# Turning the second norm's rows with VectorE squares and transfers in a transformer block on one NeuronCore

## The chip, the cores and the metric

The kernel runs on one core of a Trainium2 chip. The metric is the device time of one execution in microseconds. Three runs of the kernel before took 1683.07, 1687.08 and 1701.88 us; their median is 1687.08 us.

## What is computed

The reference is one transformer block with adaptive layer norm: attention with 32 query heads of 16 columns that share one head of keys and values, and a dense layer with relu. There are 2048 rows of 512 float32 columns and 1792 hidden columns.

```python
mod = (_silu(c) @ w_mod).reshape(c.shape[0], 6, 1, -1)
sa, ca, ga, sb, cb, gb = (mod[:, 0], mod[:, 1], mod[:, 2], mod[:, 3], mod[:, 4], mod[:, 5])
h = _layernorm(x, axis=-1) * (1 + ca) + sa
x = x + ga * _A_ref(h, A_wq, A_wk, A_wv, A_wo)     # softmax(q k^T / 4) v, then wo
h = _layernorm(x, axis=-1) * (1 + cb) + sb         # the second norm
x = x + gb * _B_ref(h, B_w1, B_w2)                 # relu(h w1) w2
```

## The kernel before

**Attention.** The main loop (`for c in range(NU * KT // 2)`, near the end of `build`) runs 256 cycles. A unit `u` is a block of 256 query rows with a group of 8 heads; there are 32 units of 16 key tiles, and a cycle takes two key tiles of one unit, so that 8 cycles are a unit and 32 cycles a block of 256 rows. In a cycle TensorE computes eight tiles of scores (`scores`, into one of three `ps_exp` banks), which ScalarE exponentiates into `pe`; eight tiles of scores of a later unit (`max_of`, into one of three `ps_max` banks), whose row maxima VectorE takes; and, at the end of each of the two parts of the cycle, the products with the values (`values`, into `ps_pv`). Once a unit, VectorE forms `negm` and its transpose `sq`, ScalarE and Pool split it (`ms`), and SP sends it through DRAM into the rows of `qp` that the next unit's scores read (`mdr<-ms`, `qp<-mdr`).

**Order.** The schedule is manual: each engine runs its instructions in the order in which the program issues them, and the strings `PARTS` give that order within the two parts of a cycle: `c` and `d` are scores, `a` and `b` maxima, `u` and `l` the work behind attention, `t` the turns. After the fourth letter of the first part the list `put_off` is run: splits on ScalarE and Pool that were put off from the cycle before.

**Work behind attention.** From the second block of cycles on, the generator `behind(b)` supplies in portions, one a cycle, what follows attention for the block before: the output projection, the second norm, the dense layer. Seven blocks are done this way; the last one comes after the loop in `behind_last`, with code of its own. Most of a portion's matmuls are issued in halves of 64 rows (`on_half`) beside the score matmuls, which use the other half of the array.

**The second norm.** For a block, `x1` holds two tiles of 128 rows. The sums of tile 0 (`ln_sums`) come during the projection. `second_norm` is stepped once a cycle, at the cycle's end, during the portions of `fill` (the second half of the dense layer of the block before; in the first block a projection of queries and four empty portions). Its first step takes the sums of tile 1 (`bn_stats`, `bn_aggr`) and starts the reciprocal square root, three operations on VectorE and 13 small ones on Pool; the second step normalises both tiles on Pool into `xn` (six operations of 128x512). Portions 4 and 5 each bring a turn: `turned_too` lets TensorE transpose four squares of 128x128 by the identity into a `ps_exp` bank, the upper halves of the rows in the first part of the cycle and the lower halves in the second (`in_two`). ScalarE copies the bank to a stage tile, and in the next cycle `split` makes its two parts `hh` (ScalarE) and `hl` (Pool), which the dense layer reads from portion 7 on.

Of the kernel before, what the change touches and what calls it, by code (L numbers as in the profile page):

```python
# [9 lines left out]
F32 = mybir.dt.float32  # L10
# [8 lines left out]
S, D, H, DH, DFF = 2048, 512, 32, 16, 1792  # L19
P = 128  # L20
LB = 512
NL = S // LB
TB = 256
NB = S // TB
TT = TB // P
DC = D // P
# [10 lines left out]

PARTS = "cbcuaucuautcuau", "tbldldladbllbld"  # L40
SYNC = mybir.DependencyInfo(mybir.DependencyClass.Sync, mybir.DependencyReason.DATA)
MANUAL = {ET.PE, ET.Activation, ET.DVE, ET.Pool, ET.SP}

# [13 lines left out]
def build(tc, nc, cst, sb, ps, dr, x, wq, wk, wv, wo, w1, w2, c, w_mod, out):  # L57
# [8 lines left out]
    def ps_fill():  # L66
        return ps.tile([P, 512], F32, name="ps_fill", tag="fill", bufs=1)
# [46 lines left out]
    cols = cst.tile([P, 2, DC], F32, name="cols")  # L114
# [91 lines left out]
    def ln_sums(mv, t, src):  # L206
        st = sb.tile([P, 6], F32, name="st", tag="st", bufs=2)
        nc.vector.bn_stats(st, src)  # L208
        nc.vector.bn_aggr(mv[:, t], st)
# [29 lines left out]
    def split(hi, lo, src, eng=None):  # L239
        nc.scalar.activation(hi, src, AF.Copy)  # L240
        (eng or nc.gpsimd).tensor_tensor(lo, src, hi.bitcast(F32), op=OP.subtract)  # L241

    def stage():
        return sb.tile([P, 512], F32, name="stg", tag="stg", bufs=3)

    def split_psum(hi, lo, pt, func=AF.Copy, stg=None, **kw):
        stg = stage() if stg is None else stg
        nc.scalar.activation(stg, pt, func, **kw)  # L248

        def parts():  # L250
            split(hi, lo, stg)

        return parts


    put_off = []
# [122 lines left out]
            qps[u].append(t.rearrange("p a n -> p (a n)"))  # L379


    later, turns = [], []

    negms = [cst.tile([P, 32], F32, name=f"negm{n}") for n in range(2)]
    for negm in negms:
# [69 lines left out]
    def turned(src, k2, pt):  # L455

        return [("turn", pt[:, (k * TT + t) * P:(k * TT + t + 1) * P],
                 src[:, t, (k2 * 2 + k) * P:(k2 * 2 + k + 1) * P])
                for k in range(2) for t in range(TT)]

    def flat(t, k2):
        return t[:, k2 * 2:k2 * 2 + 2].rearrange("p a n -> p (a n)")
# [17 lines left out]
    def normed(x1, xn, ts, nm, y, eng):  # L480
        for n, t in enumerate(ts):
            eng.tensor_scalar(xn[:, t], x1[:, t], nm[:, n:n + 1], y[:, n:n + 1],
                              op0=OP.add, op1=OP.mult)
            eng.tensor_tensor(xn[:, t], xn[:, t], cbr, op=OP.mult)
            eng.tensor_tensor(xn[:, t], xn[:, t], sbr, op=OP.add)
# [25 lines left out]
    def behind(b):  # L511
        def in_parts(todo, n):
            for i in range(0, len(todo), n):
                yield todo[i:i + n]

        def turned_too(src, parts, k2, bank):

            def turn():
                pt = bank()

                def end():
                    put_off.append(split_psum(flat(parts[0], k2), flat(parts[1], k2), pt))

                return turned(src, k2, pt), end

            turns.append(turn)

        def second(b, t):
            pt = ps_fill()
            yield from in_parts(dense2(b, t, pt), 6)  # L530
            ot = sb.tile([P, D], F32, name="ot", tag="tmp", bufs=2)
            add_psum(ot, pt, x1s[b][:, t])
            nc.sync.dma_start(out[b * TB + t * P:b * TB + (t + 1) * P], ot)

        x1, oo = open_block(b)
        if b == 0:
            qqs = [sb.tile([P, 2, LB], F32R, name="qq", tag="w1s", bufs=3) for _ in range(2)]
            rest, fill = [others_of(14 + n, qqs[n]) for n in range(2)]
            fill = itertools.chain(fill, [[]] * 4)
        else:  # L540
            rest, fill = carried.pop(), second(b - 1, 1)
        yield next(rest)
        yield next(rest)
        for k2 in range(DC // 2):
            put_off.append(partial(split, flat(oo[0], k2), flat(oo[1], k2), flat(on[b], k2)))
        yield from rest
        xn = sb.tile([P, TT, D], F32, name="xn", tag="xn", bufs=1)
        mv = ln_mv(TT)
        for t in range(TT):
            pt = ps_fill()  # L550
            for n, part in enumerate(in_parts(out_proj(pt, oo, t), 6)):
                yield part
                if t and n == 0:
                    ln_sums(mv, 0, x1[:, 0])
            add_psum(x1[:, t], pt, x1[:, t])
        ahead = [load_w1(f) for f in range(2)]

        def second_norm():
            ln_sums(mv, 1, x1[:, 1])
            stats = ln_stats(mv, TT, False)  # L560
            yield
            normed(x1, xn, range(TT), *stats, nc.gpsimd)
            yield

        norm2 = second_norm()
        hp = [sb.tile([P, DC, TB], F32R, name=n, tag="t4", bufs=2) for n in ("hh", "hl")]
        for n, part in enumerate(fill):
            if n in (4, 5):
                turned_too(xn, hp, n - 4, ps_exp)
            yield part  # L570
            next(norm2, None)
        r4 = r4s[b] = [sb.tile([P, 8, TB], F32R, name="r4", tag="big", bufs=4) for _ in range(4)]
        for f2 in range(FC // 2):
            pt = ps_fill()
            for f in range(f2 * 2, f2 * 2 + 2):
                if f + 2 < FC:
                    ahead.append(load_w1(f + 2))
                yield dense1(pt[:, (f % 2) * TB:(f % 2 + 1) * TB], ahead.pop(0), hp)
            i, f = divmod(f2 * 2, 8)
            put_off.append(split_psum(  # L580
                r4[i * 2][:, f:f + 2].rearrange("p a n -> p (a n)"),
                r4[i * 2 + 1][:, f:f + 2].rearrange("p a n -> p (a n)"), pt, AF.Relu))
        first_half = second(b, 0)
        yield from itertools.islice(first_half, 4)
        carried.append(first_half)
# [206 lines left out]

        return [back, partial(nc.gpsimd.tensor_tensor, on[b][:, g], num, den, op=OP.mult)]

    def in_two(turn):

        begun = []

        def first_part():
            begun.extend(turn())  # L800
            for d in begun[0]:
                on_half(d, 1)

        def second_part():
            for d in begun[0]:
                on_half(d, 0)
            begun[1]()

        return first_part, second_part

    def run(g):
        for _ in g:
            pass
# [71 lines left out]
    for c in range(NU * KT // 2):  # L885
        s = c * 2
        todo_of = dict(
            c=[partial(scores, *n) for n in ((s, 0), (s, 2), (s + 1, 0), (s + 1, 2))],
            d=[partial(scores, *n) for n in ((s + 2, 1), (s + 2, 3), (s + 3, 1), (s + 3, 3))
               if n[0] < NU * KT])  # L890
        if places:
            u, i, j = places.pop(0)
            todo_of.update(a=[partial(max_of, u, 0, i, j, kb) for kb in range(KB)],
                           b=[partial(max_of, u, 1, i, j, kb) for kb in range(KB)])
        for parts, load in later:
            put_off.append(parts)
            ends.append((c, load))
        later.clear()
        if not portion:

            pt = ps_fill()
            portion = [("f32r", pt, kp[:, 0:P], kp[:, 0:512], n == 0, n == 5) for n in range(6)]
        halves = [in_two(turn) for turn in turns]
        turns.clear()
        own = []
        for h in range(2):
            each = [partial(on_half, d, h) for d in portion]
            cuts = [len(each) * k // 6 for k in range(7)]
            own.append([partial(in_turn, each[x:y]) for x, y in zip(cuts, cuts[1:])])
        own[0].append(advance)  # L910
        todo_of.update(l=[partial(in_turn, own[0][k:k + 1 + k // 5]) for k in range(6)], u=own[1])
        for part in range(2):
            todo_of["t"] = [partial(in_turn, [half[part] for half in halves])]
            for n, what in enumerate(PARTS[part]):
                if todo_of.get(what):
                    todo_of[what].pop(0)()
                if part == 0 and n == 3:
                    in_turn(put_off)
                    put_off.clear()
            values(s + part)  # L920
        for due in [end for end in ends if end[0] <= c]:
            ends.remove(due)
            due[1]()  # L923
        next(todo, None)
        if c == NU * KT // 2 - 2:
            opened = open_last(NB - 1)
        if c and c % 32 == 0:
            assert next(others, None) is None
            others = behind(c // 32 - 1)
            portion = next(others)  # L930
# [31 lines left out]
```

## Time and profile before

| | before |
|---|---|
| median of three runs | 1687.08 us |
| lowest and highest run | 1683.07, 1701.88 us |
| profiled execution, its span | 1690.2 us |
| granted TensorE clock, mean | 0.994 |
| DMA, mean over the span | 77 GB/s |
| DMA packets | 88080 |

The time of the profiled execution beside its span is not given; the span is 3.1 us above the median of the runs and lies among them. In a row of the profile, `L879 PE MATMUL ps_pv<-pe,vt` is line 879 of the kernel, a matmul on TensorE that reads the tiles `pe` and `vt` and writes `ps_pv`. In the timeline a row begins with its start and its length in microseconds, `x4` says that four alike were merged, and the brackets give the idle time of the engine before the row and what ended it. PE is TensorE, DVE VectorE, ACT ScalarE, POOL GpSimd, SPq the queue from which SyncE issues transfers.

### The profile page before, as it was taken

The numbers are of one execution on the slowest core, as the hardware profiler recorded it, in microseconds if no ns is written. First come the engines' busy times: TensorE is split into PE (matmuls) and PEld (weight loads), VectorE is DVE, ScalarE is ACT, GpSimd is POOL, SyncE is SP. The second block draws the span as 40 slices with busy tenths as digits, with TensorE's granted clock in tenths as the row PEclk, the third lists the DMA queues.
The fourth block names the chain that finished last, engine by engine and source line by source line (L and its number), as shares of the span: only waits on it lengthen the run. The fifth ranks groups of instructions, "written<-read, shape, count | busy, mean of one in ns | idle before, by whom it ended". The sixth has DMA issues, their size and how long they took to land.

```text
span 1690.2 us, 34028 instructions
## 1 busy us (share of the span) xinstructions
PE 1666.9 (99%) x13130; PEld 922.0 (55%) x13130; DVE 1373.7 (81%) x2336; ACT 1228.0 (73%) x2399; POOL 345.2 (20%) x433
## 2 busy tenths in 40 slices
PE   7999999999999999999999999999999999999999
PEld 5444444445654565546654565546654565546668
DVE  7788888888888888888889888888889888888031
ACT  4238888777877778778877787778877777778830
POOL 3103355331102311121102211131103111131110
PEclk9899999999999999999999999999999999999999
DMA  8024643312301131113301131103311131103331
GB/s 288 30 62 138 199 127 102 92 60 79 101 19 48 45 104 54 36 41 96 92 25 39 47 107 49 59 17 97 91 29 35 47 115 40 61 16 100 108 121 57
DMA packets 88080, 129.86 MB, mean 77 GB/s; under 512 B 25140, under 2 KB 52724, under 8 KB 87920
## 3 DMA queue, kind: packets, MB, share of 16 engines
q1 hardware_dynamic: 86208, 127.55, 24.6%
q8 instruction: 105, 1.72, 0.4%
q14 instruction: 55, 0.45, 0.1%
q10 hardware_dynamic: 1712, 0.13, 0.1%
HBM read 100.33 MB, written 25.15 MB: 74 GB/s over the span
## 4 chain that ended last, share of the span: by engine, by line
PE 93%; DVE 3%; issue 1%; ACT 1%; DMA 1%; POOL 0%; POOLq 0%; DVEq 0%; ACTq 0%
PE ps_pv L879 30%; PE ps_exp L753 21%; PE ps_fill L163 18%; PE ps_max L426 18%; PE ps_exp L146 2%; PE ps_max L146 1%; DVE pm L428 1%; PE ps_exp L307 1%; PE ps_fill L146 1%; DVE st L208 1%; PE ps_exp L293 1%; DMA wmod<-in_w_mod_dram 1%; PE ps_exp L190 0%; PE ps_exp L159 0%; PE ps_fill L190 0%
## 5 line engine op out<-in xcount | busy, mean ns | idle before, releaser
L428 DVE TENSOR_REDUCE pm<-ps_max 128x1 f32<-128x512 f32 x2048 | 1292.5, 684 | 191.8 <-PE ps_max L426 145.6
L755 ACT ACTIVATE pe<-ps_exp 128x512 f32<-128x512 f32 x2048 | 1081.1, 605 | 301.6 <-PE ps_fill L163 137.2
L426 PE MATMUL ps_max<-kp,qp 48*128 48x512 f32 x2048 | 805.0, 439 | 7.6 <-DVE pm L428 7.5
L753 PE MATMUL ps_exp<-qp,kp 50*128 50x512 f32 x2048 | 723.7, 412 | 3.5 <-ACT pe L755 3.4
L879 PE MATMUL ps_pv<-pe,vt 128*32 128x512 f32 x4096 | 545.5, 605 | 0.0
L426 PEld LDWEIGHTS ps_max<-kp,qp 48*128 48x128 f32 x2048 | 364.0, 185 | 264.5 <-DVE pm L428 237.4
L753 PEld LDWEIGHTS ps_exp<-qp,kp 50*128 50x128 f32 x2048 | 358.7, 185 | 271.5 <-ACT pe L755 179.9
L163 PE MATMUL ps_fill<-w2r,r 64*128 64x512 f32 x1044 | 302.9, 405 | 0.0
L163 PE MATMUL ps_fill<-hh,w1s 64*128 64x256 f32 x1568 | 242.9, 285 | 0.0
L163 PEld LDWEIGHTS ps_fill<-hh,w1s 64*128 64x128 f32 x1568 | 216.9, 186 | 13.9 <-PEq L156 6.7
L163 PEld LDWEIGHTS ps_fill<-w2r,r 64*128 64x128 f32 x1044 | 180.7, 185 | 11.8 <-PEq L156 2.5
L879 PEld LDWEIGHTS ps_pv<-pe,vt 128*32 128x32 f32 x4096 | 80.6, 108 | 142.6 <-issue 122.3
L241 POOL TENSOR_TENSOR r<-stg,r 128x512 fp32r<-128x512 f32 x49 | 62.9, 1283 | 321.9 <-ACT r L240 321.9
L163 PE MATMUL ps_fill<-hT,wq 64*128 64x256 f32 x416 | 128.3, 405 | 0.0
L163 PE MATMUL ps_fill<-hl,w1s 64*128 64x256 f32 x784 | 126.4, 280 | 0.0
L163 PEld LDWEIGHTS ps_fill<-hl,w1s 64*128 64x128 f32 x784 | 105.2, 185 | 0.0
L923 POOL TENSOR_TENSOR on<-num,den 128x256 f32<-128x256 f32 x31 | 22.8, 734 | 232.5 <-DMA den<-recs 160.1
L163 PEld LDWEIGHTS ps_fill<-hT,wq 64*128 64x128 f32 x416 | 68.3, 185 | 2.8
L769 POOL COPY num<-pvs 128x256 f32<-128x256 f32 x32 | 12.7, 398 | 179.3 <-ACT pvs L765 179.3
L241 POOL TENSOR_TENSOR hl<-stg,hh 128x512 fp32r<-128x512 f32 x14 | 18.0, 1284 | 133.1 <-ACT hh L240 133.1
L261 POOL TENSOR_TENSOR x<-stg,x 128x512 f32<-128x512 f32 x14 | 18.1, 1291 | 99.2 <-ACT stg L260 99.2
L248 ACT ACTIVATE stg<-ps_fill 128x512 f32<-128x512 f32 x62 | 38.2, 616 | 0.0
(147 smaller groups left out, 927.6 us busy)
## 6 DMA issues: line engine op xcount, KB each, us to landing
w1s<-w1dr SPq DMA_DIRECT2D x104, 512.0 KB
qdr<-qq SPq DMA_DIRECT2D x48, 256.0 KB
qp<-qdr SPq DMA_DIRECT2D x128, 96.0 KB
raw<-in_B_w_dram SPq DMA_DIRECT2D x28, 256.0 KB
w1dr<-w1s SPq DMA_DIRECT2D x14, 512.0 KB
wmod<-in_w_mod_dram SPq DMA_DIRECT2D x6, 1024.0 KB
x<-in_A_x_dram SPq DMA_DIRECT2D x8, 512.0 KB
out_dram<-ot SPq DMA_DIRECT2D x16, 256.0 KB
```

The lines of the kernel that those rows point to most:

```text
L146: nc.tensor.matmul(pt, w, a, start=start, stop=stop)
L163: ins = nc.tensor.matmul(pt, w[r], a[r], start=start and h == 1, stop=stop and h == 0)
L208: nc.vector.bn_stats(st, src)
L241: (eng or nc.gpsimd).tensor_tensor(lo, src, hi.bitcast(F32), op=OP.subtract)
L248: nc.scalar.activation(stg, pt, func, **kw)
L261: nc.gpsimd.tensor_tensor(dst, stg, other, op=OP.add)
L426: nc.tensor.matmul(pt, qps[u][i][r, j * P:(j + 1) * P], kp[r, kb * 512:(kb + 1) * 512], start=True, stop=True)
L428: nc.vector.tensor_reduce(pms[u][:, (i * 2 + hf) * 4 + j, kb:kb + 1], pt, axis=AX.X, op=OP.max)
L753: nc.tensor.matmul(pt, kp[r, kt * P:(kt + 1) * P], qps[u][ct // 2][r], start=True, stop=True)
L755: nc.scalar.activation(pe, pt, AF.Exp)
L879: nc.tensor.matmul(pvt[i * 32:(i + 1) * 32], vt[:, kt], pes.pop((s, i)), start=(kt == 0), stop=(kt == KT - 1))
L923: due[1]()
```

## The change

The turns on TensorE go: `turned_too`, `in_two` and the letter `t` are taken out, and so is the copy through the stage tile. `second_norm` gets more steps, one at the end of each cycle of `fill`: `bn_stats` of tile 1; `bn_aggr` and the start of the reciprocal square root; the normalising on Pool; VectorE's transpose of tile 0; its transpose of tile 1 and the 32 transfers; the two splits, put off to the next cycle. VectorE's `transpose` turns each square of 32x32 in place, so that `xt` holds the right squares at the wrong partitions. For each tile, 16 transfers on SP's queue bring row `i` and column `j` of the squares to where they belong in `xh`: each moves 32 partitions of four pieces of 32 float32. `xh` takes the tag `xn`, which has one buffer, and `xt` the tag `tmp`, which has two.

```diff
-PARTS = "cbcuaucuautcuau", "tbldldladbllbld"
+PARTS = "cbcuaucuaucuau", "bldldladbllbld"
...
         def second_norm():
-            ln_sums(mv, 1, x1[:, 1])
+            st = sb.tile([P, 6], F32, name="st", tag="st", bufs=2)
+            nc.vector.bn_stats(st, x1[:, 1])
+            yield
+            nc.vector.bn_aggr(mv[:, 1], st)
             stats = ln_stats(mv, TT, False)
             yield
             normed(x1, xn, range(TT), *stats, nc.gpsimd)
+            yield
+            xts = [sb.tile([P, D], F32, name="xt", tag="tmp", bufs=2) for t in range(TT)]
+            for t in range(TT):
+                nc.vector.transpose(xts[t], xn[:, t])
+                if t == 0:
+                    yield
+            xh = sb.tile([P, DC, TB], F32, name="xh", tag="xn", bufs=1)
+            for t in range(TT):
+                rows = xts[t].rearrange("p (k j n) -> p j k n", k=DC, j=4)
+                cols = xh[:, :, t * P:(t + 1) * P].rearrange("p k (i n) -> p i k n", i=4)
+                for i, j in itertools.product(range(4), range(4)):
+                    nc.sync.dma_start(cols[j * 32:(j + 1) * 32, i], rows[i * 32:(i + 1) * 32, j])
+            yield
+            for k2 in range(DC // 2):
+                put_off.append(partial(split, flat(hp[0], k2), flat(hp[1], k2), flat(xh, k2)))
             yield
...
         for n, part in enumerate(fill):
-            if n in (4, 5):
-                turned_too(xn, hp, n - 4, ps_exp)
             yield part
             next(norm2, None)
...
-        halves = [in_two(turn) for turn in turns]
-        turns.clear()
...
-            todo_of["t"] = [partial(in_turn, [half[part] for half in halves])]
```

More of the change, by code (lines that the diff above doesn't have):

```diff
@@ L379, in load_q @@
             qps[u].append(t.rearrange("p a n -> p (a n)"))
-    later, turns = [], []
+    later = []
     negms = [cst.tile([P, 32], F32, name=f"negm{n}") for n in range(2)]
@@ L514, in in_parts @@
                 yield todo[i:i + n]
[L516 to L526, printed above, removed]
         def second(b, t):
@@ L793, in normalise @@
         return [back, partial(nc.gpsimd.tensor_tensor, on[b][:, g], num, den, op=OP.mult)]
[L795 to L809, printed above, removed]
     def run(g):
```

## The prediction

> **What bounds the kernel now.** First the page's busy shares and its chain of waits, columns as printed.
>
> ```profile
> span 1690.2 us, 34028 instructions
> PE 1666.9 (99%) x13130; PEld 922.0 (55%) x13130; DVE 1373.7 (81%) x2336; ACT 1228.0 (73%) x2399; POOL 345.2 (20%) x433
> PE 93%; DVE 3%; issue 1%; ACT 1%; DMA 1%; POOL 0%; POOLq 0%; DVEq 0%; ACTq 0%
> ```
>
> TensorE carries the chain. In the attention loop it, VectorE's row maxima and ScalarE's exponentials go in lockstep, so what counts is how long one cycle of the loop gets. A cycle is two parts, and each part ends with eight `ps_pv` matmuls. Next, then, the timeline of TensorE for the fourth block that runs behind attention: the `ps_pv` groups that close a cycle (start us, us, ...), and between them the turns that the change removes.
>
> ```profile
> 910.49 1.06 PE L879 MATMUL ps_pv<-pe,vt 128*32 128x512 f32 x8
> ...
> 916.49 1.06 PE L879 MATMUL ps_pv<-pe,vt 128*32 128x512 f32 x8
> ...
> 922.49 1.07 PE L879 MATMUL ps_pv<-pe,vt 128*32 128x512 f32 x8
> ...
> 929.12 1.06 PE L879 MATMUL ps_pv<-pe,vt 128*32 128x512 f32 x8
> ...
> 934.90 1.06 PE L879 MATMUL ps_pv<-pe,vt 128*32 128x512 f32 x8
> ...
> 940.68 1.06 PE L879 MATMUL ps_pv<-pe,vt 128*32 128x512 f32 x8
> ...
> 942.96 0.43 PE L159 MATMUL ps_exp<-idn,xn 64*128 64x64 f32 x4
> ...
> 947.36 1.06 PE L879 MATMUL ps_pv<-pe,vt 128*32 128x512 f32 x8
> ...
> 954.03 1.06 PE L879 MATMUL ps_pv<-pe,vt 128*32 128x512 f32 x8
> ...
> 959.82 1.06 PE L879 MATMUL ps_pv<-pe,vt 128*32 128x512 f32 x8
> ```
>
> An undisturbed cycle takes 5.78 us (934.90 to 940.68). Those that end at 947.36 and 954.03 hold the turns and take 6.68 and 6.67. The one that ends at 929.12 takes 6.63. VectorE's timeline says why:
>
> ```profile
> 911.59 0.68 DVE L208 BATCH_NORM_STATS2 st<-x 128x6 f32<-128x512 f32 x1
> 912.30 0.18 DVE L209 BATCH_NORM_AGGREGATE mv<-st 128x2 f32<-128x6 f32 x1
> ...
> 923.60 0.68 DVE L208 BATCH_NORM_STATS2 st<-x 128x6 f32<-128x512 f32 x1
> ...
> 924.94 0.17 DVE L222 TENSOR_SCALAR y<-y 128x2 int32<-128x2 int32 x1
> ...
> 948.42 0.22 DVE L432 TENSOR_REDUCE negm<-pm 128x16 f32<-128x64 f32 x1
> 948.75 0.21 DVE L392 STREAM_TRANSPOSE sq<-negm 128x32 f32<-128x32 f32 x1
> ```
>
> Both groups stand at the end of a cycle, behind its last maximum. The 0.89 us of sums at 911.59 lengthened a cycle by 0.22 us (910.49 to 916.49 is 6.00); the 1.51 us from 923.60 to 925.11 by 0.85. Both say the same: 0.66 us there is free, the rest counts in full.
>
> **What the change saves.** Eight turned squares, two copies out of PSUM and a share of an exponent bank leave each block. Their whole worth is read from the two long cycles: 6.68 + 6.67 - 2 x 5.78 = 1.79 us a block. The 1.51 us of sums become 0.68 and 0.79 us in two cycles, by the rule above 0.02 and 0.13 in place of 0.85: 0.70 saved.
>
> **What VectorE pays.** Two transposes of 128x512, of which the trace has only the 128x32 one. The two sizes of one reduction give the slope:
>
> ```profile
> L428 DVE TENSOR_REDUCE pm<-ps_max 128x1 f32<-128x512 f32 x2048 | 1292.5, 684 | 191.8 <-PE ps_max L426 145.6 <-PE ps_exp L753 36.1 <-PE ps_fill L163 6.8
> L432 DVE TENSOR_REDUCE negm<-pm 128x16 f32<-128x64 f32 x32 | 7.1, 220 | 1.1
> ```
>
> (684 - 220) / 448 is 1.04 ns a column, so an estimate of 0.21 + 480 x 1.04 ns = 0.71 us; bounds 0.21 (if columns cost nothing) and 1.42 (if a transpose passed the data twice). The first stands alone: 0.05 over what is free. The second comes behind `negm` and `sq` (948.42 to 948.96): 0.54 + 0.71 - 0.66 = 0.59. What is queued behind each on VectorE is the next cycle's first maximum, and these sums are its delay. So without any wait a block is 1.79 + 0.70 - 0.64 = 1.85 us shorter, 13 us for the seven blocks (the last block keeps its own turns). With the bounds of the transpose it is 2.4 to 0.4 us a block.
>
> **What SyncE pays.** 32 transfers a block, all on SP's queue. The tile `xh` takes the tag `xn`, which has one buffer, so its first transfer waits until both transposes have read `xn`: the transfers of tile 0 gain nothing from its earlier transpose. They start behind the second one and have to be in when ScalarE comes to the splits `hh`, one cycle later. Both ends of that lead come from ScalarE's and Pool's timelines (the wait for `xn` itself is long over: normalising ends at 935.55, one cycle later after the change, ahead of each transpose):
>
> ```profile
> 934.27 1.28 POOL L485 TENSOR_TENSOR xn<-xn,sbr 128x512 f32<-128x512 f32 x1
> ```
> ```profile
> 956.53 0.63 ACT L240 ACTIVATE hh<-stg 128x512 fp32r<-128x512 f32 x1
> ...
> 958.63 1.57 ACT L755 ACTIVATE pe<-ps_exp 128x512 f32<-128x512 f32 x3 [0.49 <-PE ps_exp L753]
> ```
>
> Start: 948.96, less what one turn cycle (0.90) and the sums (0.70) save, plus 0.05 and the transpose's 0.71: 948.12. Need: 956.53 less 1.85: 954.68. Lead: 6.6 us. Both splits now run in that one cycle; one of them left it at 5.79 (954.03 to 959.82), and the 0.49 us that ScalarE still idled a part covers most of the other: nothing counted. Now the issue, from the tile views (ns min/median/max of the issuing instruction) and SP's timeline:
>
> ```profile
> L771 SPq DMA_DIRECT2D num<-pvs x128: 523/587/1672, 159.5 to 1625.2; - x128
> L776 ACTq DMA_DIRECT2D den<-pvs x4: 589/600/601, 1623.7 to 1625.6; - x4
> L399 SPq DMA_DIRECT2D mdr<-ms x128: 302/422/1554, 93.3 to 1566.8; - x128
> L786 SPq DMA_DIRECT2D rc<-sums x31: 338/343/349, 164.7 to 1584.3; - x31
> L782 SPq DMA_DIRECT2D sums<-pvs x124: 215/251/444, 162.4 to 1583.0; - x124
> ```
> ```profile
> 919.11 2.45 SPq L771 DMA_DIRECT2D num<-pvs  x4
> 921.60 1.32 SPq L782 DMA_DIRECT2D sums<-pvs  x4
> 923.95 0.34 SPq L786 DMA_DIRECT2D rc<-sums  x1
> ...
> 952.09 1.70 SPq L399 DMA_DIRECT2D mdr<-ms  x4
> 954.96 1.12 SPq L405 DMA_DIRECT2D qp<-mdr  x4
> ```
>
> An issue takes 0.25 us from one partition to DRAM (`sums`), 0.34 from DRAM into 128 partitions, 0.42 from 16 partitions in two pieces each to DRAM (`mdr`), 0.59 from SBUF to SBUF (`num`, `den`). The new ones, 32 partitions in four pieces of 128 B, go from SBUF to SBUF: `num` is the nearest row and I take it, 2.45 us for four and the step to the next: 0.63 each. Bounds: 0.29 (`sums`) and 0.72 (`num` plus the 0.09 by which the two-piece `mdr` exceeds `rc`). A transfer lands about 1.0 us behind its issue: `rc`, which reads `sums`, starts at 923.95, 1.03 us after the last of them; after `mdr` it is 1.17.
>
> 32 x 0.63 + 1.0 = 21.2 us against a lead of 6.6: ScalarE stands 14.6 us at `hh`, with every exponential queued behind it. A few matmuls later, when the three exponent banks are full, TensorE stands too, and VectorE for lack of scores. Of ScalarE's stop, the 0.49 us that it idles anyway are not lost: 14.1 us. The packets are no second price: by the rows of the queue
>
> ```profile
> q1 hardware_dynamic: 86208, 127.55, 24.6%
> ```
>
> a packet takes 0.246 x 16 x 1690.2 / 86208 = 77 ns at a mean of 1.5 KB; 4096 on 16 engines would take 20 us at that and under 2 by bytes, beside the issue in both cases. Each transfer also waits until the eighth before it has landed, by the program's count of eight semaphores; eight issues are 5.0 us, so at 1.0 us of landing that never binds.
>
> Queued behind the 32 on SP are four `mdr` and four `qp<-mdr` transfers that the next unit's scores need: 1.70 + 1.17 + 1.12 + 1.0 = 5.0 us after the last issue. Those scores come in the second part of the next cycle, in the trace of before some 7 us after `hh`, and `hh` comes 1.0 after the last issue: in time by 3 us, whatever an issue costs. The other tiles that wait for a buffer of `xt` (`ot`; in the first block ScalarE's `stg`) come at most a cycle before or after `hh` and fall into the same stop.
>
> **The clock after the stop.** TensorE's timeline and the windows (us, busy of PE, PEld, DVE, ACT, POOL, PEclk, ...):
>
> ```profile
> 41.22 0.79 PE L426 MATMUL ps_max<-kp,qp 48*128 48x512 f32 x1 [3.47 <-DVE pm L428]
> ```
> ```profile
> 30.80:34.20 3.40, 3.38 (x4) 1.52 (x5) 3.05 (x15) 2.16 (x3) 1.52 (x2) 0.50 0.76 205
> ...
> 41.10:58.10 17.00, 16.89 (x38) 7.14 (x39) 10.52 (x19) 4.13 (x6) 0.95 (x2) 0.50 0.17 63
> ```
>
> After an idle stretch of 3.47 us the clock was granted at 0.50, for 17.0 us though TensorE was busy 16.89 of them; an earlier spell lasted 3.4 us. A stop of 14 us will bring one. I take the short spell, half of 3.4 us: 1.7 a block; bounds 0 and 8.5. [...]
>
> Sum: 7 x (14.1 + 1.7 - 1.85) = 98 us on a profiled span of 1690.2, or 1788. That span lies 3.1 us above the median of the runs, 1687.1, so for a run: **1785 us**.
>
> **Rivals.** (1) An issue costs what `mdr` does, 1.70 / 4 and the step of 0.04, 0.465: the stop falls by 32 x 0.165 = 5.3 us a block, 37 in all: 1748. For it: 32 whole-quadrant partitions may be simpler than `num`'s 16 at an offset; against it: `mdr` goes to DRAM. [...]
> (2) Issues at the price of `rc` or `sums`, 0.38 or 0.29 with the step: 7 x 8.0 or 7 x 10.9 us less, 1729 or 1709, and under 1697 where the stop is too short for the clock.
> (3) The other side: the transfers are in before `hh`. That needs 32 issues in 5.6 us, under 0.175 us each, below the fastest row (0.215), or SP starting a cycle earlier, which the one buffer forbids. Then only the 13 us remain: 1674, 0.8% faster.
> (4) The long clock spell, or issues over 0.8 us: 1833.
>
> **How the numbers follow.** Forecast 0.60, (1) 0.18, (2) 0.09, (3) 0.04, (4) 0.09. The range takes in the forecast with 0.72 us an issue (+20 us) and a second clock window, most of (4) at the top, and (1) with 0.42 at the bottom: 1735 to 1832, leaving out (2) and (3) and the tail of (4). A measurement of this kernel can tell 1% from no change, 1670 to 1704 here: (3) and the cheapest of (2) fall within it, 0.05, faster 0.02, slower 0.93.
>
> **What would show it.** Right: rows `xh<-xt` on SP at about 0.6 us, back to back for 20 us in seven places; a wait of `hh` for a DMA of some 14 us, seven times; no L159 turns in the loop and no 6.67 us cycles; transposes near 0.7 us; a mean granted clock below the 0.994 of before. Wrong: issues under 0.3 us, `xh` rows starting right behind the first transpose, or idle stretches of TensorE in those cycles that end on something other than `hh`.

## The result and the profile after

Four runs of the changed kernel took 1795.12 to 1809.76 us, median 1803.63; the kernel before, 1683.07 to 1701.88, median 1688.57. The ratio is 1.0658, 95% interval 1.0605 to 1.0711: 6.6% slower. The forecast was 1785 us in a range from 1735 to 1832.

The page of the changed kernel, its head, its chain of waits and one of its groups:

```profile
span 1802.1 us, 34032 instructions
PE 1673.0 (93%) x13018; PEld 922.2 (51%) x13018; DVE 1379.1 (77%) x2350; ACT 1221.2 (68%) x2385; POOL 344.7 (19%) x433
...
PE 86%; SPq 7%; DVE 3%; ACT 1%; issue 1%; DMA 1%; POOL 0%; POOLq 0%; DVEq 0%; ACTq 0%
...
L240 ACT ACTIVATE hh<-xh 128x512 fp32r<-128x512 f32 x14 | 8.0, 621 | 111.2 <-DMA xh<-xt 79.7
```

The span grew by 111.9 us, and ScalarE stood 111.2 us idle ahead of 14 splits. TensorE's share fell from 99% to 93%, and SP's queue, which had no part in the chain before, now has 7% of it. (Of the 111.2 us the full list of groups puts 31.5 down to `mdr<-ms`, which `hh` does not read: those transfers share the queue and its semaphores, eight by the trace, with `xh<-xt`.)

The timelines of VectorE, SP, ScalarE and TensorE for the fourth block behind attention, the one that the prediction reads (brackets: idle before, and what ended it):

```profile
994.13 0.22 DVE L432 TENSOR_REDUCE negm<-pm 128x16 f32<-128x64 f32 x1
994.45 0.21 DVE L392 STREAM_TRANSPOSE sq<-negm 128x32 f32<-128x32 f32 x1
994.66 0.71 DVE L557 STREAM_TRANSPOSE xt<-xn 128x512 f32<-128x512 f32 x1
```
```profile
995.39 21.56 SPq L565 DMA_DIRECT2D xh<-xt  x32
1017.06 1.92 SPq L399 DMA_DIRECT2D mdr<-ms  x4
1020.13 1.12 SPq L405 DMA_DIRECT2D qp<-mdr  x4
```
```profile
1000.89 1.09 ACT L759 ACTIVATE pe<-ps_exp 128x512 f32<-128x512 f32 x2 [0.64 <-PE ps_max L426]
1018.34 1.15 ACT L240 ACTIVATE hh<-xh 128x512 fp32r<-128x512 f32 x2 [16.37 <-DMA xh<-xt]
```
```profile
1003.55 0.40 PE L163 MATMUL ps_fill<-w2r,r 64*128 64x512 f32 x1
1020.03 0.79 PE L757 MATMUL ps_exp<-qp,kp 50*128 50x512 f32 x1 [16.09 <-ACT pe L759]
```

The 32 issues begin 0.02 us behind the second transpose and take 21.56 us. ScalarE comes to `hh` at 1001.97 (1018.34 less 16.37), 6.6 us after the transpose ended, and stands until 1.39 us after the last issue. TensorE goes on for some 2 us, until the exponent banks are full, and stops for 16.09. The windows around the stop (us, busy of PE, PEld, DVE, ACT, POOL, granted clock, DMA share, GB/s):

```profile
995.00:1003.90 8.90, 8.50 (x64) 3.72 (x60) 7.96 (x14) 4.78 (x11) 0.25 (x1) 1.00 0.14 21
1003.90:1020.00 16.10, 0.04 (x2) 0.00 (x0) 0.53 (x1) 1.66 (x4) 0.95 (x1) 0.61 0.17 24
1020.00:1024.40 4.40, 4.37 (x20) 1.97 (x20) 1.89 (x3) 3.03 (x6) 2.67 (x3) 0.50 0.01 4
1024.40:1030.20 5.80, 5.80 (x62) 3.68 (x58) 4.89 (x8) 4.13 (x8) 0.18 (x1) 1.00 0.42 141
```

In the stop the clock goes down (0.61 on the mean), and the first 4.4 us behind it run at half of it (0.50).

Taking the start of the last `ps_pv` matmul of each cycle in both traces gives the length of every cycle, and the difference after minus before, as a mean over the seven blocks (cycles counted from the block's first):

| cycle of the block | what is in it | us |
|---|---|---|
| 9, 10 | sums of tile 1 in two cycles in place of one | -0.83, +0.22 |
| 12 | first turn gone; tile 0's transpose ahead of it | -0.86 |
| 13 | second turn gone, tile 1's transpose added | -0.26 |
| 14, 15 | the stop at `hh` and what follows | +17.29, +0.59 |
| all others together | | -0.2 |

They add up to 16 us a block. (In one cycle of the first block the trace of before is 2 us longer, which every other trace here lacks, that of the kernel with the split sums alone too, though one of them only in part; it is the -0.2, and no part of the change.)

### The profile page after: what moved, and what is told of

Same layout as the page of the kernel before. It is cut to its first block, busy times and chain, and to the rows that moved or that the text cites. A ratio compares the mean times of both kernels' runs of the same rounds, so it can differ in the third digit from the quotient of the medians.

```text
span 1802.1 us, 34032 instructions
## 1 busy us (share of the span) xinstructions
PE 1673.0 (93%) x13018; PEld 922.2 (51%) x13018; DVE 1379.1 (77%) x2350; ACT 1221.2 (68%) x2385; POOL 344.7 (19%) x433
## 4 chain that ended last, share of the span: by engine, by line
PE 86%; SPq 7%; DVE 3%; ACT 1%; issue 1%; DMA 1%; POOL 0%; POOLq 0%; DVEq 0%; ACTq 0%
PE ps_pv L867 27%; PE ps_exp L757 19%; PE ps_fill L163 17%; PE ps_max L426 16%; SPq L565 7%; PE ps_exp L146 2%; DVE pm L428 1%; PE ps_max L146 1%; PE ps_exp L307 1%; PE ps_fill L146 1%; PE ps_fill L137 1%; DMA xh<-xt 1%; PE ps_exp L293 0%; PE ps_exp L190 0%; ACT hh L240 0%
## 5 line engine op out<-in xcount | busy, mean ns | idle before, releaser
L757 PE MATMUL ps_exp<-qp,kp 50*128 50x512 f32 x2048 | 726.4, 414 | 111.2 <-ACT pe L759 111.1
L867 PE MATMUL ps_pv<-pe,vt 128*32 128x512 f32 x4096 | 551.6, 611 | 0.0
L163 PE MATMUL ps_fill<-w2r,r 64*128 64x512 f32 x1044 | 308.7, 411 | 0.0
L163 PEld LDWEIGHTS ps_fill<-w2r,r 64*128 64x128 f32 x1044 | 185.8, 188 | 11.7 <-PEq L156 2.5
L240 ACT ACTIVATE hh<-xh 128x512 fp32r<-128x512 f32 x14 | 8.0, 621 | 111.2 <-DMA xh<-xt 79.7
L241 POOL TENSOR_TENSOR hl<-xh,hh 128x512 fp32r<-128x512 f32 x14 | 17.6, 1278 | 157.9 <-DMA mdr<-ms 113.0
```

What stands on the lines that cost most here:

```text
L163: ins = nc.tensor.matmul(pt, w[r], a[r], start=start and h == 1, stop=stop and h == 0)
L757: nc.tensor.matmul(pt, kp[r, kt * P:(kt + 1) * P], qps[u][ct // 2][r], start=True, stop=True)
L867: nc.tensor.matmul(pvt[i * 32:(i + 1) * 32], vt[:, kt], pes.pop((s, i)), start=(kt == 0), stop=(kt == KT - 1))
```

## The experiments

The theory: the stop is 32 issues on SP's queue, one behind the other, less a lead of 6.6 us; and each block pays that stop, some microseconds of half clock behind it, and gains 1.73 us. The rivals: VectorE or Pool is late; bytes or packets set the time; the clock costs nothing. The kernels with half as many transfers, with one piece, with a buffer of its own and with all of it one cycle earlier were run once each, so that their part of the argument rests on one trace apiece. "Cycles 14 and 15" are those of the table above, as means over the seven blocks.

**Without the transfers.** The splits read the squares where VectorE left them:

```diff
-                for i, j in itertools.product(range(4), range(4)):
-                    nc.sync.dma_start(cols[j * 32:(j + 1) * 32, i], rows[i * 32:(i + 1) * 32, j])
...
-                put_off.append(partial(split, flat(hp[0], k2), flat(hp[1], k2), flat(xh, k2)))
+                put_off.append(partial(split, flat(hp[0], k2), flat(hp[1], k2), xts[k2]))
```

> Left out: the 32 transfers a block; the splits read the transposed squares at the partitions where VectorE left them. Theory (the stop of ScalarE at hh is the transfers' alone): the cycles with the stop lose it, and what remains is the change's saving, 1.73 us a block by the difference of the two traces cycle by cycle (0.61 for the sums, 1.77 for the turns, 0.65 paid for the second transpose): a span of 1676 to 1679, ratio to before 0.993. Rival (VectorE's transposes or Pool's later normalising hold the splits up): a wait at hh stays, and the span stays over 1780.

1677.17 us, ratio 0.9937 (0.9906 to 0.9969). ScalarE no longer waits at the splits, and cycles 14 and 15 are as before the change; what remains is -0.84, +0.23, -0.86 and -0.32, 1.79 us a block. The profiled span was 1669.5, since the cycles ahead of the first block took 6.3 us less in that execution. So the transposes and the later normalising hold nothing up, and the transfers are the whole of the loss.

**Half as many transfers.** The same bytes in 16 transfers, in pieces of twice the length:

```diff
-                rows = xts[t].rearrange("p (k j n) -> p j k n", k=DC, j=4)
+                rows = xts[t].rearrange("p (k i n) -> p i k n", k=DC, i=2)
...
-                for i, j in itertools.product(range(4), range(4)):
-                    nc.sync.dma_start(cols[j * 32:(j + 1) * 32, i], rows[i * 32:(i + 1) * 32, j])
+                for i, j in itertools.product(range(2), range(4)):
+                    nc.sync.dma_start(cols[j * 32:(j + 1) * 32, i], rows[j * 32:(j + 1) * 32, i])
```

> The same bytes in 16 transfers a block, each of 32 partitions in four pieces of 256 B; the squares do not come to their own places. Theory (each issue on SP costs 0.67 us whatever it carries): 16 x 0.674 + 1.3 - 6.6 = 5.5 us of stop in place of 16.4, the span 1802 - 7 x 10.9 = 1726. Rival (bytes moved set the time): 1802.

1731.66 us, a span of 1729.9, 4 us over the expectation. The tile views of the changed kernel and of this one show the issue at its old price (ns min/median/max), and the group of splits its wait:

```profile
L565 SPq DMA_DIRECT2D xh<-xt x224: 586/599/1495, 380.6 to 1630.7; - x112
```
```profile
L565 SPq DMA_DIRECT2D xh<-xt x112: 589/600/1250, 380.4 to 1558.3; - x112
L240 ACT ACTIVATE hh<-xh 128x512 fp32r<-128x512 f32 x14 | 8.0, 621 | 39.4 <-DMA mdr<-ms 28.6 <-DMA xh<-xt 10.7
```

ScalarE waited 39.4 us in the seven blocks, 5.6 each where 5.5 were expected. Bytes are not the price. (The pieces are halved here too, 2048 a block in place of 4096; the next kernel takes them alone.)

**The same number, a fourth of the pieces.** 32 transfers of one piece of 512 B:

```diff
...
+                    nc.sync.dma_start(xh[j * 32:(j + 1) * 32, i, t * P:(t + 1) * P],
+                                      xts[t][i * 32:(i + 1) * 32, j * P:(j + 1) * P])
```

> The same 32 transfers a block with the same bytes, each of 32 partitions in one piece of 512 B, which are a fourth of the packets; the squares do not come to their own places. Theory (the issue counts, and pieces add little to it): 0.59 to 0.60 us an issue, by the rows of num, 0.62 to 0.67 with the step; a stop of 14.6 to 16.4 us, a span of 1790 to 1802. Rival (4096 small packets a block set the time): a fourth of it, no stop, a span under 1690.

1797.36 us, a span of 1795.3. SP's and ScalarE's timelines in the fourth block:

```profile
990.47 20.92 SPq L563 DMA_DIRECT2D xh<-xt  x32
```
```profile
1007.68 0.63 ACT L240 ACTIVATE hh<-xh 128x512 fp32r<-128x512 f32 x1 [10.63 <-DMA xh<-xt]
1012.67 0.63 ACT L240 ACTIVATE hh<-xh 128x512 fp32r<-128x512 f32 x1 [4.36 <-DMA xh<-xt]
```

The issues take nearly as long with a fourth of the pieces, 1024 a block: 20.9 us against 21.6 in this block, 0.589 us each at the median against 0.599. Here the two splits read different transfers and wait one after the other, 10.63 and 4.36 us. The pieces are not the price either; the count of issues is.

**A buffer of its own for tile 0's half.**

```diff
-            xh = sb.tile([P, DC, TB], F32, name="xh", tag="xn", bufs=1)
+            xhs = [sb.tile([P, DC, P], F32, name="xh", tag=("xh", "xn")[t], bufs=1) for t in range(TT)]
...
-                put_off.append(partial(split, flat(hp[0], k2), flat(hp[1], k2), flat(xh, k2)))
...
+                put_off.append(partial(split, hp[0][:, :, ts], hp[1][:, :, ts], xhs[t]))
```

The splits go by tile here, so that the first one reads tile 0's half alone.

> Tile 0's half of xh gets a buffer of its own, so that its 16 transfers need not wait until the second transpose has read xn. Theory (one buffer holds all 32 back): xh rows start right behind the first transpose, 6.5 us earlier; 16 issues of 0.674 us fill that lead, so the stop falls from 16.4 to 9.9 us and the span by 7 x 6.5 = 45 us to 1757. Rival (SP was busy or the squares were not ready, the buffer did not matter): start and span as they were, 1802.

1757.64 us, a span of 1755.6. VectorE's and SP's timelines:

```profile
969.00 0.70 DVE L557 STREAM_TRANSPOSE xt<-xn 128x512 f32<-128x512 f32 x1
975.44 0.71 DVE L557 STREAM_TRANSPOSE xt<-xn 128x512 f32<-128x512 f32 x1
```
```profile
969.73 21.61 SPq L565 DMA_DIRECT2D xh<-xt  x32
```

The issues now begin behind the first transpose, 6.4 us ahead of the second, and take no less time. ScalarE's wait came down from 111.2 to 65.9 us in all, 6.5 a block. The shared buffer had held all 32 back.

**All of it one cycle earlier.** The sums of tile 1 in one cycle again, the splits where they were:

```diff
             nc.vector.bn_stats(st, x1[:, 1])
-            yield
             nc.vector.bn_aggr(mv[:, 1], st)
...
             yield
+            yield
             for k2 in range(DC // 2):
```

> The changed kernel with the sums of tile 1 in one cycle again, so that normalising, transposes and transfers all come one cycle earlier and the splits where they are. Theory: the lead grows by 5.8 us, the stop falls from 16.4 to 10.6; the sums cost 0.61 us a block more, and the second transpose no longer stands behind negm, 0.65 less: 1802 - 7 x 5.8 = 1761. Rival (Pool is not done with xn by then): the transposes wait, and less is gained.

1768.63 us, a span of 1766.8. ScalarE's wait came down to 73.0 us in all, 10.4 a block:

```profile
L240 ACT ACTIVATE hh<-xh 128x512 fp32r<-128x512 f32 x14 | 8.0, 621 | 73.0 <-DMA xh<-xt 39.9 <-DMA mdr<-ms 33.1
```

Cycles 14 and 15 cost 12.4 us in place of 17.9, 2.0 more than the wait, as in the changed kernel (17.9 with a wait of 15.9). The span is 6 us over the expectation: the issues took 21.3 us on the mean in this execution (21.0 in the changed kernel's), and the cycles ahead of the first block 3.7 us more than in the trace of before, which has nothing to do with the edit.

**The sums alone.** The kernel before, with the sums of tile 1 over two cycles and the turns on TensorE:

```diff
-            ln_sums(mv, 1, x1[:, 1])
+            st = sb.tile([P, 6], F32, name="st", tag="st", bufs=2)
+            nc.vector.bn_stats(st, x1[:, 1])
+            yield
+            nc.vector.bn_aggr(mv[:, 1], st)
```

> The kernel before with only the second part of the change: the sums of tile 1 over two cycles, the turns on TensorE as they were. Theory (0.66 us of VectorE is free at a cycle's end): 0.61 us a block less, 4 us in all, ratio 0.9975; the cycle that took 6.63 us takes 5.80 and the next one 6.00. Rival (a cycle later for the normalising delays the turns): the turn cycles get longer than 6.67 us and the gain goes.

1685.31 us, ratio 0.9977 (0.995 to 1.0003). By the runs alone this is not told from no change. The cycles show it: -0.82 and +0.23 in six of the seven blocks (+0.58 in one), turn cycles as long as before.

**TensorE kept busy in the stop.** Idle products ahead of the place where it stops; first 30, then 66:

```diff
             values(s + part)
+            if part == 0 and c >= 32 and c % 32 == 14:
+                pt = ps_max()
+                for _ in range(66):
+                    nc.tensor.matmul(pt, kp[:, 0:P], kp[:, 0:512], start=True, stop=True)
```

> The changed kernel with 30 idle products of 128x512 on TensorE, some 12 us, ahead of the place where it stops in each block, written to a spare bank that nobody reads. Theory (of the 17.9 us by which the stop's two cycles are longer, 16.4 are ScalarE's stop and some 1.5 the half clock after it): the stop stays, the clock stays near 0.99, and the span falls by up to 10 us, to 1792 to 1798. Rival (the 1.5 us are ScalarE's refilling of the exponent banks): 1802 as it was, at a higher clock.

1805.24 us, ratio 1.0677 (1.0628 to 1.0726): no gain. A product took 0.24 us, not 0.40; TensorE still stood 9.03 us, and the clock went to half as before (0.974 on the mean; eight `ps_pv` behind the stop took 1.90 us, not 1.06), against the expectation. It decided nothing, so:

> As e9, with 66 idle products in place of 30: at the 0.236 us that one took there, 15.6 us, so that TensorE has no idle stretch over 1 us left while ScalarE stands (in e9 9 us were left, and the clock still went to half). Theory (of the cost of the stop's two cycles beyond ScalarE's own wait, 1.5 us is the half clock after it): no spell at half clock, a mean clock of 0.99, ScalarE's wait at hh still near 16 us, the part behind it some 1.5 to 1.8 us shorter: a span 10 to 12 us under the changed kernel's, 1790 to 1793. Rival (ScalarE's refilling is the cost): the clock stays up and the span does not fall.

1794.29 us, ratio 1.0610 (1.0582 to 1.0637), a span of 1792.0 and a mean clock of 0.993. The ratios of this kernel and of the changed one overlap; the cycles tell them apart. The windows of the fourth block (columns as above: the loop before, the idle products, the end of the stop, the next cycle):

```profile
985.00:999.80 14.80, 14.41 (x103) 7.25 (x102) 12.34 (x21) 8.02 (x17) 0.25 (x1) 1.00 0.11 16
999.80:1013.40 13.60, 13.60 (x62) 10.99 (x60) 0.00 (x0) 0.00 (x0) 0.00 (x0) 1.00 0.17 24
1013.40:1016.80 3.40, 2.28 (x18) 1.20 (x19) 1.57 (x3) 3.33 (x7) 2.53 (x2) 1.00 0.05 7
1016.80:1022.60 5.80, 5.80 (x61) 3.69 (x62) 4.91 (x9) 4.49 (x10) 1.29 (x1) 1.00 0.41 136
```

ScalarE waited 0.7 us a block longer, behind issues of 21.6 us on the mean:

```profile
L240 ACT ACTIVATE hh<-xh 128x512 fp32r<-128x512 f32 x14 | 8.0, 622 | 115.9 <-DMA xh<-xt 66.4 <-DMA mdr<-ms 49.4
```

That is 16.6 a block, and cycles 14 and 15 cost 16.9: 0.3 more than the wait. In the changed kernel they cost 2.0 more. The difference, 1.7 us a block, is the half clock. The span came out as expected in part by luck: of the 10.1 us by which it fell, 3.5 lie ahead of the first block, where the edit does nothing, and 6.6 in the seven blocks, 0.9 each.

**Through DRAM.** For each tile four transfers write the squares in the order of `xh`, and one of 128 partitions reads them back:

```diff
...
+            xd = dr.tile([TT, 4, 32, DC, 4, 32], F32, name="xd", tag="xd", bufs=2)
             for t in range(TT):
                 nc.vector.transpose(xts[t], xn[:, t])
+                rows = xts[t].rearrange("p (k j n) -> p k j n", k=DC, j=4)
+                for i in range(4):
+                    nc.sync.dma_start(xd[t, :, :, :, i].rearrange("j c k n -> c k j n"), rows[i * 32:(i + 1) * 32])
...
+                nc.sync.dma_start(xh[:, :, t * P:(t + 1) * P], xd[t].rearrange("j c k i n -> (j c) k (i n)"))
```

> The squares go through DRAM: for each tile four transfers write them in the order in which xh needs them, and one of 128 partitions reads the tile back, ten transfers a block in place of 32; the writes of tile 0 start behind its own transpose. Theory (count and price of the issues decide): behind the second transpose 4 x 0.47 + 1.2 for the landing + 0.34 + 0.39 + 1.3 = 5.1 us, inside the lead of 6.6: no stop, a span of 1676 to 1679, ratio 0.993. Rival (128-byte pieces to DRAM, or the second trip, cost more than the issues): a stop of some us at hh, each us 7 us of span.

1694.39 us, ratio 1.0028 (0.9996 to 1.0061): the rival, in part. The tile view and ScalarE's timeline:

```profile
L561 SPq DMA_DIRECT2D xd<-xt x56: 569/628/1063, 371.9 to 1513.4; - x56
L566 SPq DMA_DIRECT2D xh<-xd x14: 547/568/1849, 380.1 to 1515.7; - x14
```
```profile
763.66 1.15 ACT L240 ACTIVATE hh<-xh 128x512 fp32r<-128x512 f32 x2 [0.81 <-DMA xh<-xd]
...
953.17 1.15 ACT L240 ACTIVATE hh<-xh 128x512 fp32r<-128x512 f32 x2 [2.53 <-DMA xh<-xd]
```

The issues cost 0.63 and 0.57 us, not the 0.47 and 0.34 expected, and ScalarE still waits 0.8 to 2.8 us a block. The seven blocks fall in two sorts. In four, with waits of 0.77 to 1.03 us, the clock stayed up, and cycle 14 got 0.91 to 1.17 us longer: the whole wait and 0.12 to 0.14 more. In the other three, with waits of 2.33 to 2.75, the clock stood at half for 3.4 us behind the wait, and cycles 14 and 15 cost 1.4 to 1.7 us more than the wait. So the half clock shows its price here without any idle product. With one cycle more of lead ScalarE should not wait:

**Through DRAM, one cycle earlier.** Both edits together.

> Through DRAM as in e6, and one cycle earlier as in e5. Theory: what e6 still waited at hh, 0.8 to 2.8 us a block, is less than the 5.8 us that the earlier cycle gives: no stop, and all of the saving of e1 remains, 1.75 us a block: a span of 1669 to 1677, ratio 0.993. Rival (the sums in one cycle cost their 0.61 us and nothing else is gained): as the change without transfers less 4 us, ratio 0.996.

1677.04 us, ratio 0.9922 (0.9900 to 0.9944): 0.8% faster than the kernel before, and faster than the changed one; 1.75 us a block as expected. Its group of splits, where the changed kernel stood 111.2 us:

```profile
L240 ACT ACTIVATE hh<-xh 128x512 fp32r<-128x512 f32 x14 | 8.1, 632 | 0.0
```

The profiled execution had a span of 1683.9, because its clock stood at half for 41.0 us near the start; the spans of the other five lie between 1674.0 and 1679.9. The seven blocks are each 1.7 to 1.8 us shorter than in the trace of before (3.7 in the first, which holds the odd 2 us).

## Why the prediction was right

The mechanism came out as forecast, in the place forecast: 32 issues behind one another on SP's queue, ScalarE held at `hh`, TensorE stopped behind it, and half clock after that. The sizes, per block:

| term | forecast, us | measured, us |
|---|---|---|
| saved by the turns, the sums, less the transposes | 1.85 | 1.73 (1.79 without the transfers) |
| 32 issues | 20.2 | 21.0, mean of seven (20.6 to 21.8) |
| landing | 1.0 | 1.4 |
| lead | 6.6 | 6.6 |
| ScalarE's wait at `hh` | 14.6 | 15.9 |
| what TensorE loses beside that wait | -0.5 | +0.3 |
| half clock | 1.7 | 1.7 |

- **VectorE.** The transpose took 0.70 us at the median and 0.71 beside `sq`, as estimated from two reductions, though no row had tied a transpose to a reduction's slope. The rule that 0.66 us at a cycle's end is free held within 0.1 us in each case: the split sums (0.22 against 0.13 for the second), tile 0's transpose (0.03 against 0.05), tile 1's behind `negm` and `sq` (some 0.6 against 0.59).
- **The one buffer.** Read off the code, confirmed by the issue that starts behind the second transpose and by the 45 us of ScalarE's wait that a buffer for tile 0 gave back.
- **The price of an issue.** `num` was the right row: 0.599 us at the median against 0.587. The reason given for it was not, and to that extent the choice was luck. The forecast put the price down to both sides lying in SBUF; through DRAM the writes cost 0.63 and the reads 0.57, about the same. With the step to the next, an issue took 0.66 (21.0 / 32); the 0.63 of the forecast is 0.62 by the row of `num` that it cites (2.49 us for four). Rival 1, at the price of `mdr`, would have been 1748 us, and the runs exclude it.
- **ScalarE's own idle time.** This step failed, by 0.8 us a block: 0.49 us of the wait was counted as absorbed. It is not. The wait cost 0.3 us more than its length with TensorE kept busy, and the short waits of the kernel through DRAM 0.12 to 0.14 more. The forecast had drawn on the same idle time for the second split in that cycle, which without the transfers indeed costs only 0.02 us. A likely reason, read from the timeline and not tested by itself: TensorE needs not only the end of the wait (1018.34) but the two splits (to 1019.49) and an exponential behind them before a bank is free (1020.03).
- **The clock.** The short spell was nearer than the long one, and the price of 1.7 us came out as forecast, but partly by luck: the half clock lasted 4.3 to 5.1 us beyond TensorE's return in all seven blocks, not 3.4, and half of that would be 2.2 to 2.6. What makes up the rest stays open. Half clock for 17.0 us with TensorE at work, the row from the start of the kernel before, did not come back behind any of the stops. The second clock window that the range allows for was the author's estimate, and no run shows it: each stop of the changed kernel has one spell, of 17.07 us.
- **What is queued behind on SP.** `mdr` and `qp<-mdr` came late and in time, as forecast: no scores waited for them beyond the stop.

In all 15.9 + 0.3 + 1.7 - 1.73 = 16.2 us a block, 113 in seven, less the odd 2 us: the 111.9 of the two spans. The forecast's 98 was short by the issues and landings (1.3 us a block), by ScalarE's idle time (0.8) and by a saving 0.1 too large.

## What to carry to other kernels

Moving work from a busy engine to transfers traded its time for issues here, 1.73 us saved a block for 21.0 us of 32 issues: count them, take the price of one from the nearest rows of the trace, and set their sum, with the landing, against the time between the last producer and the first reader, not against the work that was removed. A reader that waited in ScalarE's queue, 16.37 us in the fourth block, stopped everything behind it, here the whole loop: TensorE stood 16.09 us. What helped was fewer issues (10 in place of 32, the first four behind tile 0's own transpose) and one cycle more of lead, and each alone was not enough (1694.39 and 1768.63 us; together 1677.04).

## What had not been expected

- An issue on SP costs 0.59 to 0.63 us for forms as different as one piece of 512 B within SBUF (0.589), four pieces of 128 B within SBUF (0.599) and a write of 128-byte pieces to DRAM (0.628), while the `mdr` writes of before cost 0.42 and reads into 128 whole rows 0.34. What sets the step between them stays open.
- The spells of half clock lasted 17.07 us in the changed kernel, most of the stop included, and 6.83, 10.24 or 13.65 us where the stop was shorter, all multiples of 3.41 us; the mean granted clock was 0.960 in the changed kernel, 0.968 one cycle earlier, 0.973 with a buffer of its own and 0.980 with half as many transfers. They ended 3.3 to 6.7 us behind TensorE's return in these traces (4.3 to 5.1 in the changed kernel), however long the stop had been.
- The read back from DRAM landed 2.6 to 4.3 us after the end of its issue, against 1.4 us for transfers within SBUF, both taken up to the start of the split that waited for them.
